# The first two x tiles of a fused attention and FFN kernel: transposed by DMA instead of on TensorE

## The chip, the cores and the metric

The kernel runs on one core of one Trainium2 chip. Its time is the device time of one execution in microseconds. Before the change three runs took 249.02, 248.76 and 249.07 us, a median of 249.02 us.

## The reference

The input `x` has 2048 rows of 1024 bf16 values. Two blocks work on it, and a gate per row mixes their results:

```
g   = sigmoid(sum(x * gate_w))                      # one number per row
qkv = x @ wqkv                                      # 1024 -> 3 * 1024, 32 heads of 32
pq, pk = phi(q), phi(k)                             # phi(t) = (t + 1 if t > 0 else exp(t)) + 1e-6
kv  = sum over rows of pk^T v, z = sum over rows of pk      # per head
a   = (pq @ kv / (pq . z + 1e-6)) @ wo              # linear attention
i   = argmax over rows of x @ w_r
b   = x, with sigmoid(x[i] @ w_r) * ((silu(x[i] @ w_gate) * (x[i] @ w_up)) @ w_down) added to row i
out = g * a + (1 - g) * b
```

So K and V are needed for all rows before any output can be made, and one single row goes through the FFN.

## The kernel before

The 2048 rows are 16 tiles of 128 (`NT`), the 1024 columns of `x` are 8 chunks of 128 (`KC`). TensorE contracts over the partitions, so every product with `wqkv` needs `x` transposed: `xT[p, c, s]` holds column `128 c + p` of row `s`. For K and V a 128x128 block of `xT` is the stationary operand and 512 (K) or about 350 (V) columns of the weights `wkv` stream past it. For Q it is the other way round.

The order of the stages:

1. Start-up: `wkv` comes in row by row of chunks. `load_k(c)` brings the K columns of chunk c, 256 KB each. The first two x tiles are worked on with the K rows as these arrive: `first_mm(t, c, c + 1)` makes the two 512-column matmuls (`first` in the profile) of tile t with K row c. The loop below `first_mm(0, 0, 1)` goes over c and alternates: row c for tile 0, then row c - 1 for tile 1.
2. `unit_V(t, 2)`: the last third of V, together with the two router columns (`w_r` and `gate_w`, put into `wkv` by way of the tile `wps`), for tiles 0 to 3 and then, after K of tile 2, for tiles 4 to 15.
3. From tile 4 on, a loop of K, the rest of V, and Q for later tiles; the sums over rows (`unit_KVACC`), the FFN of the one selected row, and at the end the output tiles.

Who brings x where it is needed: tiles 0 and 1 are loaded as they are by `load_x` (a plain DMA of 256 KB each, to `xnat`) and transposed on TensorE by `unit_T`. That makes eight 128x128 transposes per tile into two PSUM tiles (`pst`), and copies one of these to `xT` on VectorE (DVE) and one on ScalarE (ACT). Tiles 2 and 3 each come by one DMA that transposes on the way (`sp.dma_start_transpose`), tiles 4 to 15 by three such DMAs of four tiles each.

What sets the order: the kernel is written with a tile framework that puts in the semaphores. `in_order` (lines 78 to 90) wraps the calls of an engine, so that instructions keep the order of the program on TensorE, DVE, ACT and SP. The wrapper is why most lines of the profile read L83, and tiles are told apart by their names. All large loads are issued by SP in this order: x tile 0, x tile 1, K rows 0 to 7, the last third of V for all chunks in one DMA (640 KB, behind `v_cut`), the transposing DMAs of tiles 2, 3, 4-7, 8-11 and 12-15, the rest of V in two DMAs, and the Q weights. From K row 4 on, an issue also waits until an earlier DMA has landed, since their landing semaphores are used in turn: K row 7 and the V third wait for the load that SP issued eight DMAs earlier. ACT issues two small loads of 2 KB for the router columns at the start.

While TensorE waits for data it runs dummy matmuls on a constant (`warm`, tile `warm_ps`): six of 512 columns at the start (`N_WARM`), two of 128 behind `wps`, four of 128 behind the second `unit_T`. Their result is not used. The start-up on TensorE is written out like this:

```
unit_T(0)
wps = ...                       # router columns: transpose, copy into wkv
warm(2, 128)
unit_T(1)
warm(4, 128)
first_mm(0, 0, 1)
for c in range(1, KC):
    first_mm(0, c, c + 1)
    if c < KC - 1:
        first_mm(1, c - 1, c)
```

Of the kernel before, what the change touches and what calls it, by code (L numbers as in the profile page):

```python
# [13 lines left out]
BF = mybir.dt.bfloat16  # L14
# [8 lines left out]
P = 128  # L23
S = 2048
D = 1024
F = 3584
NT = S // P
KC = D // P
NG = D // P
EPS = 1e-6  # L30
LN1EPS = math.log1p(EPS)
N_WARM = 6
Q_PER_T = {4: 2, 5: 1, 6: 1, 7: 2, 8: 2, 9: 1, 10: 2, 11: 1, 12: 1, 13: 1, 14: 1, 15: 1}
VH = (11, 11, 10)
REDUCE_AFTER = {(6, 3): 0, (9, 4): 1}
# [10 lines left out]
def kernel(  # L46
# [14 lines left out]
    x2d = A_x.rearrange("b s d -> (b s) d")  # L61
    out2d = out.rearrange("b s d -> (b s) d")
    wqkv_v = A_wqkv.rearrange("(c p) n -> p c n", p=P)
    x_v = x2d.rearrange("(t p) d -> p t d", p=P)
# [13 lines left out]
    def in_order(engine, names, own=(False,)):  # L78
        last = [None]

        def wrap(fn):
            def call(*a, **k):
                inst = fn(*a, **k)  # L83
                if last[0] is not None and (strict[0] or own[0]):
                    tc.add_manual_dep(inst.ins, last[0].ins.name, NOSYNC, reason="program order on this engine")
                last[0] = inst
                return inst

            return call

        return SimpleNamespace(**{n: wrap(getattr(engine, n)) for n in names})

    pe = in_order(nc.tensor, ["matmul", "transpose"])
    dve = in_order(nc.vector, ["memset", "tensor_copy", "tensor_scalar", "tensor_scalar_add", "tensor_tensor", "scalar_tensor_tensor",
                               "reciprocal", "max", "max_index", "tensor_reduce", "stream_shuffle"], strict_dve)
    sp = in_order(nc.sync, ["dma_start", "dma_start_transpose"])
    act = in_order(nc.scalar, ["activation", "copy"])
# [11 lines left out]
    xT = pa.tile([P, KC, S], BF)  # L109
# [6 lines left out]
    ps_t = ps_t_cm.__enter__()  # L116
# [5 lines left out]
    xin_cm = tc.tile_pool(name="xin", bufs=2)  # L122
    xin = xin_cm.__enter__()
    wrg_rows = xin.tile([16, P], BF, name="wrg_rows", bufs=1)
    xnat = {}

    def load_x(t0, n):
        xt4 = xin.tile([P, n, D], BF, name=f"xnat{t0}", bufs=1)
        sp.dma_start(out=xt4[:, 0:n, :], in_=x_v[:, t0 : t0 + n, :])
        for i in range(n):  # L130
            xnat[t0 + i] = xt4[:, i, :]

    def load_k(c):
        sp.dma_start(out=wkv[:, c, 0:D], in_=wqkv_v[:, c, D : 2 * D])

    load_x(0, 1)
    load_x(1, 1)
    for c in range(KC):
        load_k(c)
    v_cut = D + 32 * (VH[0] + VH[1])  # L140
    sp.dma_start(out=wkv[:, :, v_cut : 2 * D], in_=wqkv_v[:, :, D + v_cut : 3 * D])
# [9 lines left out]
    ident = const.tile([P, P], BF)  # L151
# [34 lines left out]
    def phi_exp(ps):  # L186
        u = tmp.tile([P, 512], F32, tag="phi_u")
        act.activation(u[:], ps, ACTF.Relu, scale=-1.0, bias=LN1EPS)
        e = tmp.tile([P, 512], F32, tag="phi_e")
        act.activation(e[:], u[:], ACTF.Exp, scale=-1.0, bias=LN1EPS)  # L190
        return e

    def phi_dve(ps, e0, out_ap):
        dve.scalar_tensor_tensor(out_ap, ps, EPS, e0[:], op0=ALU.max, op1=ALU.add)

    def phi_evac(ps, out_ap):
        phi_dve(ps, phi_exp(ps), out_ap)

    def unit_T(t):
        for h, eng in enumerate((dve.tensor_copy, act.copy)):  # L200
            pst = ps_t.tile([P, 512], BF, tag="t")
            for c in range(4):
                pe.transpose(pst[:, c * P : (c + 1) * P], xnat[t][:, (4 * h + c) * P : (4 * h + c + 1) * P], ident[:])
            eng(xT[:, 4 * h : 4 * h + 4, t * P : (t + 1) * P], pst[:].rearrange("p (c s) -> p c s", c=4))

    pk_t = {}
    vt_t = {}
# [1 line left out]
    def kv_open(t):  # L209
        if t not in pk_t:  # L210
            pk_t[t] = kvp.tile([P, D], BF, tag="pk", name=f"pk{t}")
            vt_t[t] = kvp.tile([P, VH[0] + VH[1], 33], BF, tag="vt", name=f"vt{t}")
            nc.gpsimd.memset(vt_t[t][:, :, 32:33], 1.0)  # L213

    def kv_mm(ps, t, nb, c0, c1):
        for c in range(c0, c1):
            pe.matmul(ps[:], lhsT=xT[:, c, t * P : (t + 1) * P], rhs=wkv[:, c, 512 * nb : 512 * nb + 512],
                             start=(c == 0), stop=(c == KC - 1))
# [43 lines left out]
    def warm(n, w=512):  # L262
        for _ in range(n):
            pe.matmul(warm_ps[:, 0:w], lhsT=warm_w, rhs=warm_x[:, 0:w], start=True, stop=True)

    warm(N_WARM)
    kv_open(0)
# [3 lines left out]
    def first_mm(t, c0, c1):  # L271
        for c in range(c0, c1):
            for nb in range(2):
                kv_mm(first[t][nb], t, nb, c, c + 1)

    unit_T(0)
    wps = ps_t.tile([P, 16], BF, tag="t")
    pe.transpose(wps[:], wrg_rows[:], ident[0:16, 0:16])
    dve.tensor_copy(wkv[:, :, 2 * D : 2 * D + 2], wps[:].rearrange("p (w c) -> p c w", w=2))
    warm(2, 128)  # L280
    unit_T(1)
    warm(4, 128)
    first_mm(0, 0, 1)
    for c in range(1, KC):
        first_mm(0, c, c + 1)
        if c < KC - 1:
# [455 lines left out]
```

## Time and profile before

| | us |
|---|---|
| median of 3 runs | 249.02 |
| the profiled execution | 249.02 |
| its span, first to last instruction | 247.4 |
| TensorE busy (matmuls) | 241.0 (97%) |
| VectorE (DVE) busy | 172.7 (70%) |
| ScalarE (ACT) busy | 127.7 (52%) |
| GpSimd (POOL) busy | 52.7 (21%) |
| DMA moved | 47.78 MB, mean 193 GB/s |

The profile is one execution, recorded by the hardware. A line of instructions gives the line of the kernel, the engine, the operation, the tiles (out<-in), how many, and times. PE is TensorE's matmuls, PEld its weight loads, which run beside them. "SPq" is the queue of SP, which only issues DMAs; of a DMA the trace gives when it was issued, how long the issue held the queue, and how long after the issue it had landed. The chain is the work that ended last, followed back step by step to whatever released it. The packets of the core's 16 DMA engines are recorded one by one, so the rate in any stretch can be asked for. Matmuls overlap in the pipeline: a single one's duration (379 ns for 512 columns) is longer than the distance from one start to the next, and it is this distance, the pitch, that tells TensorE's pace.

### The profile page before, as it was taken

What the parts mean: (1) busy time and instruction counts of PE and PEld (TensorE: products, weight loads), DVE (VectorE), ACT (ScalarE), POOL (GpSimd) and SP (SyncE); (2) the same over time, 40 slices, a digit from 0 to 9 for tenths busy, and PEclk for the clock granted to TensorE, in tenths of its full rate; (3) what the DMA queues carried; (4) which work ended last, traced back from release to release, by engine and by line L of the source; (5) the groups of instructions that cost most, each with busy time, mean ns of one, the idle gap of its engine ahead of it and who ended that gap; (6) DMA issues with size and microseconds to landing.
All of it is one profiled execution on the core that took longest, in us unless ns stands there. A gap on an engine that the chain in (4) does not pass through costs nothing.

```text
span 247.4 us, 4873 instructions
## 1 busy us (share of the span) xinstructions
PE 241.0 (97%) x1901; PEld 124.3 (50%) x1926; DVE 172.7 (70%) x264; ACT 127.7 (52%) x215; POOL 52.7 (21%) x100
## 2 busy tenths in 40 slices
PE   8999999999999999999999999999999999999994
PEld 4466756654554554554554555544443444444442
DVE  1053124379985979845989999996789999954342
ACT  3095344455566466545555555668887633333300
POOL 6000000400000100000013300101666689950000
PEclk9999999999999999999999999999999999999999
DMA  6999994499969993599659891000003654565122
GB/s 212 339 243 200 273 396 127 106 337 335 269 193 300 342 290 79 153 326 391 205 164 455 286 243 48 3 4 21 0 3 127 200 184 149 152 190 168 47 83 86
DMA packets 46311, 47.78 MB, mean 193 GB/s; under 512 B 16776, under 2 KB 35472, under 8 KB 46224
## 3 DMA queue, kind: packets, MB, share of 16 engines
q1 hardware_dynamic: 45648, 46.28, 61.0%
q0 software_dynamic: 608, 1.19, 1.8%
q8 instruction: 15, 0.25, 0.4%
q14 instruction: 8, 0.07, 0.1%
q10 hardware_dynamic: 32, 0.00, 0.0%
HBM read 39.33 MB, written 8.39 MB: 193 GB/s over the span
## 4 chain that ended last, share of the span: by engine, by line
PE 97%; issue 1%; DVE 0%; DVEq 0%
PE ps L83 88%; PE first L83 3%; PE kvacc L83 2%; PE warm_ps L83 1%; PE red L83 1%; PE pst L83 1%; PE dps L83 1%; PE pm L83 1%; DVE ot L83 0%; PE yps L83 0%; DVEq L737 0%; PE pt L83 0%; PE hps L83 0%; PE rps L83 0%; PE wps L83 0%
## 5 line engine op out<-in xcount | busy, mean ns | idle before, releaser
L83 PE MATMUL ps<-wkv,xT 128*128 128x352 bf16 (+2 forms) x600 | 106.1, 334 | 0.4
L83 PEld LDWEIGHTS <-xT 128*128 128x128 bf16 x640 | 62.3, 98 | 49.3 <-issue 0.5
L83 ACT ACTIVATE u<-ps 128x512 f32<-128x512 f32 x60 | 35.9, 598 | 46.4 <-PE ps L83 46.2
L83 PE MATMUL ps<-xT,wq 128*128 128x512 bf16 x246 | 57.6, 379 | 0.7 <-issue 0.3
L83 PE MATMUL ps<-m_sb,pq_all 128*128 128x512 bf16 (+2 forms) x258 | 55.1, 372 | 0.4 <-issue 0.2
L83 ACT ACTIVATE e<-u 128x512 f32<-128x512 f32 x64 | 40.3, 630 | 2.1
L83 PEld LDWEIGHTS <-pq_all 128*128 128x128 bf16 x264 | 25.4, 98 | 30.2 <-issue 0.7
L640 POOL TENSOR_TENSOR pq_all<-pq_all,rb 128x512 bf16<-128x512 bf16 x32 | 36.5, 1170 | 12.1 <-DVE rb L83 11.7
L83 PEld LDWEIGHTS <-wq 128*128 128x128 bf16 x256 | 24.4, 98 | 28.4 <-issue 1.4
L83 DVE SCALAR_TENSOR_TENSOR gacc<-wt,hcol,gacc 128x1024 f32<-128x1024 bf16 x27 | 34.5, 1279 | 0.4
L83 DVE SCALAR_TENSOR_TENSOR ot<-ps,gate,xg 128x512 bf16<-128x512 f32 (+2 forms) x33 | 24.0, 738 | 14.3 <-PE ps L83 14.2
L83 DVE SCALAR_TENSOR_TENSOR gacc<-wt,xs_f,gacc 128x2048 f32<-128x2048 bf16 x14 | 32.8, 2345 | 0.2
L83 ACT ACTIVATE xg<-xt,omg 128x1024 f32<-128x1024 bf16 x16 | 18.1, 1146 | 26.8 <-DVE ot L83 25.9
L83 DVE SCALAR_TENSOR_TENSOR pq_all<-ps,e 128x512 bf16<-128x512 f32 x32 | 21.9, 686 | 11.3 <-ACT e L83 11.3
L83 DVE SCALAR_TENSOR_TENSOR pk<-ps,e 128x512 bf16<-128x512 f32 x28 | 19.0, 686 | 11.8 <-ACT e L83 11.8
L83 DVE STREAM_SHUFFLE rb<-rdp 128x512 f32<-128x512 f32 x32 | 22.8, 752 | 0.0
L83 ACT CAST vt<-ps 128x352 bf16<-128x352 f32 x32 | 14.4, 454 | 11.4 <-PE ps L83 11.1
L213 POOL MEMSET vt<- 128x22 bf16 x16 | 3.8, 440 | 75.7 <-PE kvacc L83 75.3
L83 ACT CAST vc<-ps 128x320 bf16<-128x320 f32 x16 | 6.5, 429 | 7.3 <-PE ps L83 7.3
L83 DVE COPY rg<-ps 128x2 f32<-128x2 f32 x16 | 2.5, 159 | 10.2 <-ACT vc L83 10.1
L355 POOL DMA_DIRECT2D xs<-in_A_x_dram x1 | 0.7, 711 | 39.5 <-DVE sig L83 39.5
L83 DVE SCALAR_TENSOR_TENSOR pk<-first,e 128x512 bf16<-128x512 f32 x4 | 2.8, 692 | 9.0 <-ACT e L83 9.0
(100 smaller groups left out, 96.1 us busy)
## 6 DMA issues: line engine op xcount, KB each, us to landing
wt<-in_B_w_down_dram SPq DMA_DIRECT2D x14, 512.0 KB, 4.6
wt<-in_B_w_gate_dram SPq DMA_DIRECT2D x8, 512.0 KB, 7.6
wt<-in_B_w_up_dram SPq DMA_DIRECT2D x8, 512.0 KB, 7.4
xt<-xp SPq DMA_DIRECT2D x16, 256.0 KB, 2.7
out_dram<-ot SPq DMA_DIRECT2D x15, 256.0 KB, 2.0
wt<-in_B_w_gate_dram SPq DMA_DIRECT2D x8, 384.0 KB, 8.0
wt<-in_B_w_up_dram SPq DMA_DIRECT2D x8, 384.0 KB, 6.9
wkv<-in_A_wqkv_dram SPq DMA_DIRECT2D x8, 256.0 KB, 4.6
```

The lines of the kernel that those rows point to most:

```text
L83: inst = fn(*a, **k)
L213: nc.gpsimd.memset(vt_t[t][:, :, 32:33], 1.0)
L355: nc.gpsimd.dma_start(out=xs8[:], in_=x2d[bass.ds(idx_val, 1), :].rearrange("o (c p) -> (o c) p", p=P))
L640: nc.gpsimd.tensor_tensor(sl, sl, rb[:], op=ALU.mult)
```

## The change

The first two x tiles also come by transposing DMAs (`load_xt`), straight into `xT`; `load_x`, `xnat` and `unit_T` are gone. SP's order becomes: x tile 0, K row 0, x tile 1, K rows 1 to 7, and then as before. On TensorE the 16 transposes and the four dummies behind them are gone, `N_WARM` is 8 instead of 6, and the two matmuls of K row 0 with tile 0 stand ahead of the `wps` transpose and its two small dummies. The copies from PSUM to `xT` on DVE and ACT are gone as well.

```diff
-N_WARM = 6
+N_WARM = 8
...
-    def load_x(t0, n):
-        xt4 = xin.tile([P, n, D], BF, name=f"xnat{t0}", bufs=1)
-        sp.dma_start(out=xt4[:, 0:n, :], in_=x_v[:, t0 : t0 + n, :])
-        for i in range(n):
-            xnat[t0 + i] = xt4[:, i, :]
...
-    load_x(0, 1)
-    load_x(1, 1)
-    for c in range(KC):
+    def load_xt(t):
+        sp.dma_start_transpose(out=xT[:, :, t * P : (t + 1) * P], in_=x2d[t * P : (t + 1) * P, :])
+
+    load_xt(0)
+    load_k(0)
+    load_xt(1)
+    for c in range(1, KC):
         load_k(c)
...
-    def unit_T(t):
-        for h, eng in enumerate((dve.tensor_copy, act.copy)):
-            pst = ps_t.tile([P, 512], BF, tag="t")
-            for c in range(4):
-                pe.transpose(pst[:, c * P : (c + 1) * P], xnat[t][:, (4 * h + c) * P : (4 * h + c + 1) * P], ident[:])
-            eng(xT[:, 4 * h : 4 * h + 4, t * P : (t + 1) * P], pst[:].rearrange("p (c s) -> p c s", c=4))
...
-    unit_T(0)
+    first_mm(0, 0, 1)
     wps = ps_t.tile([P, 16], BF, tag="t")
     pe.transpose(wps[:], wrg_rows[:], ident[0:16, 0:16])
     dve.tensor_copy(wkv[:, :, 2 * D : 2 * D + 2], wps[:].rearrange("p (w c) -> p c w", w=2))
     warm(2, 128)
-    unit_T(1)
-    warm(4, 128)
-    first_mm(0, 0, 1)
     for c in range(1, KC):
         first_mm(0, c, c + 1)
         if c < KC - 1:
```

More of the change, by code (lines that the diff above doesn't have):

```diff
@@ L124 @@
     wrg_rows = xin.tile([16, P], BF, name="wrg_rows", bufs=1)
-    xnat = {}
-    def load_x(t0, n):
-        xt4 = xin.tile([P, n, D], BF, name=f"xnat{t0}", bufs=1)
-        sp.dma_start(out=xt4[:, 0:n, :], in_=x_v[:, t0 : t0 + n, :])
-        for i in range(n):
-            xnat[t0 + i] = xt4[:, i, :]
     def load_k(c):
         sp.dma_start(out=wkv[:, c, 0:D], in_=wqkv_v[:, c, D : 2 * D])
-    load_x(0, 1)
-    load_x(1, 1)
-    for c in range(KC):
+    def load_xt(t):
[4 more added lines that the diff above has]
+    for c in range(1, KC):
         load_k(c)
```

## The prediction

> **What bounds the kernel now.** First the page: busy times and the chain that ended last.
>
> ```profile
> PE 241.0 (97%) x1901; PEld 124.3 (50%) x1926; DVE 172.7 (70%) x264; ACT 127.7 (52%) x215; POOL 52.7 (21%) x100
> ...
> PE 97%; issue 1%; DVE 0%; DVEq 0%
> ```
>
> TensorE is busy for 241.0 of 247.4 us and is 97% of the chain. Its matmul stream has no holes to speak of, so the end can move only by TensorE's start-up, by a new hole, or by its pace. All edits lie in the start-up, so the chain in order of time comes next (start, length, what):
>
> ```profile
> 0.98 0.04 issue
> 1.02 2.72 PE warm_ps L83 x6
> 3.74 1.01 PE pst L83 x8
> 4.75 0.12 PE wps L83
> 4.88 0.33 PE warm_ps L83 x2
> 5.20 0.85 PE pst L83 x8
> 6.06 0.43 PE warm_ps L83 x4
> 6.48 4.37 PE first L83 x20
> ```
>
> Two things are to be seen. Up to 6.48 us TensorE does only dummies and transposes: filler until the first K rows have landed. And its pace changes there: a 512-column dummy takes 2.72/6 = 0.45 us, a 512-column `first` matmul 4.37/20 = 0.218; a 128-column dummy 0.43/4 = 0.107, about half the 0.218 instead of a quarter. The array thus runs at half rate until about 6.5 us, after some 5.4 us of unbroken work, and at full rate from then on. (The clock column of the page shows full speed there too; the pitch is the better witness.)
>
> The stretches for the `first` matmuls alone (length, busy time, count):
>
> ```profile
> 6.28:6.80 0.52, 0.52 (x2) 0.00 (x0) 0.00 (x0) 1.00 1.18 323
> 6.80:13.28 6.48, 6.43 (x30) 0.00 (x0) 0.60 (x1) 1.00 1.10 322
> ```
>
> K row 0 takes two matmuls, to 6.80; from row 1 on, 30 matmuls run back to back at 6.48/30 = 0.216 us, and after 13.28 the V matmuls follow without a hole. When row 1 may start therefore sets the end of the kernel. The DMA issues tell when it may (issue to landing in us, one issue per line; issue times from the timeline: x tile 0 at 0.98, x tile 1 at 1.45, K row 0 at 1.91, K row 1 at 2.40, the last third of V at 5.76):
>
> ```profile
> xnat<-in_A_x_dram SPq DMA_DIRECT2D x1, 256.0 KB, 2.7
> ...
> xnat<-in_A_x_dram SPq DMA_DIRECT2D x1, 256.0 KB, 2.9
> ...
> wkv<-in_A_wqkv_dram SPq DMA_DIRECT2D x1, 256.0 KB, 3.8
> ...
> wkv<-in_A_wqkv_dram SPq DMA_DIRECT2D x1, 256.0 KB, 4.3
> ...
> wkv<-in_A_wqkv_dram SPq DMA_DIRECT2D x1, 640.0 KB, 7.1
> ```
>
> So x0 lands at 3.7, x1 at 4.35, K row 0 at 5.7, K row 1 at 6.7, 0.1 us before TensorE takes it at 6.80, and the V third at 12.9, 0.4 us before 13.28. The start-up is bound by one stream of bytes, x0, x1, K0, K1, and the transposes are hidden in its wait.
>
> **The change, part by part.** *Removed from TensorE:* 16 transposes (1.01 + 0.85 us of chain), four 128-column dummies (0.43). *Added:* two 512-column dummies. All of it is at half rate and before row 1. The eight dummies end at 1.02 + 8 x 0.43 = 4.5 us. *Row 0* moves ahead of the small `wps` transpose and needs only x0 and K0, no more x1. All this is worth nothing while K row 1 is the last to come: the 30 matmuls behind it take 6.48 us in either kernel. The most that row 0's own two matmuls can give is the 0.1 us between the landing at 6.7 and 6.80. The four copies out of PSUM (two on DVE, two on ACT) were on nobody's path: zero; their cover is the idle 7.6 us of DVE and 5.7 us of ACT before their first K work.
>
> *The x tiles by DMA transpose.* K1 now comes behind x0 (transposed), K0, x1 (transposed). It is the same 1 MB, so what counts is how fast it flows. The rows of the same trace where transposes flow, begin and end (windows 2 to 6, 12.25 to 12.75, 26.5 to 27.5, 27.6 to 28.8 and 29 to 32 us):
>
> ```profile
> DMA packets 698, 1.25 MB, mean 312 GB/s; under 512 B 91, under 2 KB 91, under 8 KB 698
> ...
> DMA packets 192, 0.05 MB, mean 98 GB/s; under 512 B 192, under 2 KB 192, under 8 KB 192
> ...
> DMA packets 1134, 0.29 MB, mean 290 GB/s; under 512 B 1134, under 2 KB 1134, under 8 KB 1134
> ...
> DMA packets 188, 0.13 MB, mean 108 GB/s; under 512 B 110, under 2 KB 188, under 8 KB 188
> ...
> DMA packets 824, 1.14 MB, mean 379 GB/s; under 512 B 16, under 2 KB 824, under 8 KB 824
> ```
>
> (a) Transposes in full flow move 290 GB/s in 256-byte packets: 0.90 us for a tile of 0.262 MB. Plain loads made 312 in this same start-up (0.84 us) and 379 at their best (0.69). Two tiles: +0.13 to +0.43 us; I take 0.2, nearer to the start-up's own row.
> (b) Going from plain loads to transposes, the stream fell to 98 GB/s for 0.5 us: 0.33 us lost against 290. After the change this happens once, K0 to x1: 0 to 0.33, I take 0.1, because there it fell into a full queue.
> (c) Going from transposes back to plain loads it fell to 108 GB/s for 1.2 us: 0.13 MB where 379 GB/s takes 0.34 us, 0.86 us lost. This happens twice ahead of K1 (x0 to K0, x1 to K1): 0 to 1.7 us. That row stands behind 3 MB of transposes and mine behind a quarter of one each, so I take half, 0.4 each, 0.8.
> (d) SP's issue. A plain issue takes 0.45 us. The two 128-row transposes took 4.05 and 1.76 us, behind a full queue. With an empty queue one costs between a plain 0.43 and 1.76. At 1.76, K1 is issued at 0.98 + 2 x 1.76 + 0.45 + three steps of 0.05 = 5.1 instead of 2.40, and with the shortest delay shown for 256 KB (2.7) lands at 7.8. This runs beside (a) to (c) and is not added: it only sets a floor of 7.8 at its upper end.
>
> Sum: 0.2 + 0.1 + 0.8 = 1.1, K1 lands at 7.8 instead of 6.7; less the 0.1 us of slack, row 1 starts 1.0 us late. Bounds: +0.1 - 0.1 = 0.0 at the low end, 0.43 + 0.33 + 1.72 - 0.1 = +2.4 at the high end.
>
> The Trainium skill speaks against the change: "VectorE: DVE Perf Modes", The three transpose paths, gives 1309 ns for one 128x128 block by DMA and 390 ns on TensorE, and its rules send a transpose whose result may go to PSUM to TensorE. A tile is eight blocks; one after the other that would be an estimated 10.5 us each, and K1 some 19 us late. This trace moves a tile in 0.90 us once transposes flow, so I don't expect that figure to hold here.
>
> *Queued behind.* On SP stand K2 to K7, the V third, then the transposes of the other x tiles; the later issues wait for landings of the earlier ones (K7's for K0, the third of V for x1). All were issued 4 to 7 us before they landed, so 1 us more of issue is covered. Their landings shift with the stream by about 1.1, their deadlines on TensorE by 1.0: the third of V keeps 0.3 of its 0.4 us, the transpose of x tiles 4 to 7 (issued 12.64, 7.8 to landing, 20.4, needed at 21.10) about 0.6. Zero, but thin. K rows land every 0.7 us and are used up every 4 x 0.216 = 0.86, so rows 2 to 7 do not bind.
>
> *The clock.* Before, TensorE worked without a pause from 1.02 until the pitch doubled near 6.5. After, it pauses from 4.5 until K0 is there (about 5.3: without x1 ahead, with (a) and (c) once), works for about 1.3 us and waits again until 7.8. If the pauses do not put the doubling off, this costs nothing, since row 1 starts later than 6.5: taken as 0. If the unbroken work has to begin anew at 7.8, full rate comes 5.4 us later and half of that is lost: +2.7 us. This is the upper bound.
>
> The Trainium skill, "TensorE: Matmul & The Clock Gate", Part 1, has the gate open after about 3.4 us of sustained work in a free-running window; eight dummies of 0.43 us just fill one. By that rule the clock may come as early as 4.5 us or as late as a further window of 3.4 us, an estimated loss of up to 1.7. The row, 5.4 us from first work to full pitch, fits a window that began at 3.0.
>
> **Total.** The profiled run took 249.02 us, the median of the three runs as well, with a span of 247.4 (1.6 lie around it). 249.02 + 1.0 = 250.0.
>
> **Rivals.**
> 1. *Clock late.* The pauses cost a further window of half rate: 1.0 plus 1.4 to 2.7, about 251.4 to 252.7. For it: nothing shows the clock rising over a pause. Against it: two thirds of the time to 6.5 stays busy.
> 2. *The issue binds, not the stream.* SP needs 1.76 us per transpose, (b) and (c) are small, and K1 lands at 7.8 by its issue alone: 250.0 again, but with idle DMA engines at 3 to 5 us. For it: the shortest transpose issue on record. Against: that one stood behind a full queue.
> 3. *Hidden anyway.* From an empty queue the transposes flow at once, nothing is lost at the turns, K1 lands at 6.8: 249.0 to 249.4.
> 4. *Faster.* K1 lands earlier than now. Before, the first microsecond of the stream ran at 260 GB/s, and K1's landing came a microsecond after its bytes' turn at the mean rate, which tells of engines out of step. If transposes keep them in step, K1 could land at 6.1 and row 1 start 0.6 us early: 248.4. It decides if K1 lands before 6.3. Against: the same bytes in smaller packets.
>
> **How the numbers follow.** Mine 0.36, the clock 0.26, issue 0.13, hidden 0.18, faster 0.07. About 0.5 us (0.2%) is what a measurement of this kernel tells from no change. Slower by more: 0.30 of mine (it reaches below 249.5 at its low bounds), all of the clock, 0.12 of issue, 0.05 of hidden, 0.73; within: 0.20; faster: 0.07. The range reaches from hidden (249.0) to most of the clock case (252.4). Without the clock case and the two that gain or hide it would be 249.3 to 251.4.
>
> **What would show it.** Right: no `pst` on TensorE, two holes in it before row 1 (near 4.5 to 5.3 and 6.3 to 7.8), K1 landing at 7.4 to 8.2, then a pitch of 0.216 and the V matmuls from about 14.3 without a hole. A pitch of 0.43 after row 1 shows rival 1; SP issues of 1.5 us or more and idle DMA engines rival 2; K1 at 6.8 rival 3. Wrong above all would be a first transpose with a set-up cost of its own, which no row here shows, or a hole at the third of V or at x tiles 4 to 7.

## The result, and the profile after

The changed kernel is slower: 255.08 us, the median of four runs (254.47 to 255.52), against 248.98 us (248.76 to 249.07). The ratio is 1.0245, with a 95% interval of 1.0219 to 1.0271, or +6.1 us. The prediction was 250.0 with a range up to 252.4: right in direction, far too small. The profiled execution took 255.52 us; its span is 254.0 where it was 247.4, so 6.6 us have to be found.

The page of the changed kernel, busy time of TensorE and the engines' shares of the chain:

```profile
PE 242.5 (95%) x1884; PEld 123.1 (48%) x1908; DVE 171.9 (68%) x262; ACT 126.6 (50%) x213; POOL 52.6 (21%) x100
...
PE 94%; DMA 2%; SPq 1%; issue 1%; DVE 0%; DVEq 0%
```

TensorE has 17 fewer recorded matmuls and is busy for 1.5 us more. The chain now has 2% of DMA and 1% of SP's queue in it, which were not there. Both point at the start-up, so the chain of the changed kernel in order of time (start, length, what):

```profile
0.98 1.36 SPq L83
2.35 0.06 issue
2.41 0.56 SPq L83
2.97 0.05 issue
3.02 1.24 SPq L83
4.26 0.04 issue
4.31 5.22 DMA wkv<-in_A_wqkv_dram
9.53 0.04 issue
9.57 9.23 PE first L83 x30
18.80 4.59 PE ps L83 x33
```

TensorE no longer starts this chain. SP does: 1.36 us to issue the transpose of x tile 0, 0.56 for K row 0, 1.24 for the transpose of x tile 1, so that K row 1 is issued at 4.31 instead of 2.40. It lands at 9.53 instead of 6.7. Then the 30 `first` matmuls behind it, as the stretches of the changed kernel for these alone show (length, busy time and count on TensorE, DVE and ACT, the clock, DMA share, GB/s):

```profile
9.57:14.86 5.29, 5.29 (x13) 0.00 (x0) 0.00 (x0) 0.50 1.21 307
14.86:18.64 3.78, 3.78 (x18) 0.00 (x0) 0.60 (x1) 1.00 1.05 235
```

They take 9.07 us instead of 6.48: up to 14.86 one starts every 0.42 us, from there every 0.22 (the one on the border is counted in both stretches). V starts at 18.64 instead of 13.28. One more piece lies far from the change. TensorE's timeline of the changed kernel (start, length, what, the idle time before in brackets):

```profile
90.36 0.39 PE L83 MATMUL ps<-xT,wq 128*128 128x512 bf16 x1
91.86 1.47 PE L83 MATMUL ps<-xT,wq 128*128 128x512 bf16 x6 [1.12 <-issue]
```

The same seven matmuls in the timeline of the kernel before stand in one piece:

```profile
84.89 1.90 PE L83 MATMUL ps<-xT,wq 128*128 128x512 bf16 x7
```

In the middle of a group of eight accumulating matmuls for Q, right behind the 128 short matmuls of `unit_KVACC` for tiles 4 to 7, TensorE stands still for 1.12 us (one of the eight has no record in either profile). The releaser is given as issue: it waits for no semaphore.

The account is then, measured as the shift of the same instructions against the kernel before:

| piece | us |
|---|---|
| row 1 starts at 9.57 instead of 6.80 | +2.77 |
| half clock in the `first` matmuls, 9.07 instead of 6.48 | +2.59 |
| hole at 90.75 (the shift goes from 5.36 to 6.53 across it) | +1.17 |
| sum, of 6.6 in the span | +6.53 |

### The profile page after: what moved, and what is told of

Same layout as the page of the kernel before. It is cut to its first block, busy times and chain, and to the rows that moved or that the text cites. A ratio compares the mean times of both kernels' runs of the same rounds, so it can differ in the third digit from the quotient of the medians.

```text
span 254.0 us, 4831 instructions
## 1 busy us (share of the span) xinstructions
PE 242.5 (95%) x1884; PEld 123.1 (48%) x1908; DVE 171.9 (68%) x262; ACT 126.6 (50%) x213; POOL 52.6 (21%) x100
## 4 chain that ended last, share of the span: by engine, by line
PE 94%; DMA 2%; SPq 1%; issue 1%; DVE 0%; DVEq 0%
PE ps L83 85%; PE first L83 4%; DMA wkv<-in_A_wqkv_dram 2%; PE kvacc L83 2%; SPq L83 1%; PE red L83 1%; PE dps L83 1%; PE pm L83 1%; DVE ot L83 0%; PE yps L83 0%; DVEq L723 0%; PE pt L83 0%; PE hps L83 0%; PE rps L83 0%; PE xs_ps L83 0%
## 5 line engine op out<-in xcount | busy, mean ns | idle before, releaser
L83 DVE SCALAR_TENSOR_TENSOR ot<-ps,gate,xg 128x512 bf16<-128x512 f32 (+2 forms) x33 | 23.9, 735 | 14.3 <-PE ps L83 14.2
L83 PE MATMUL first<-wkv,xT 128*128 128x512 bf16 x32 | 9.8, 475 | 4.1 <-DMA wkv<-in_A_wqkv_dram 4.1
```

## The experiments

Three questions follow: why K row 1 lands so late, what costs the clock, and where the hole comes from. The edits are against the changed kernel or the one before, as said. Each ratio is against runs of the kernel before on the same chip; its medians there were 249.13 (runs e1 to e4), 249.12 (e5 to e8) and 249.43 (e9 to e12). What the profiles show, in us:

| kernel | K1 issued | K1 landed | row 1 starts | half rate until | V starts | hole | span |
|---|---|---|---|---|---|---|---|
| before | 2.40 | 6.7 | 6.80 | 6.5 | 13.28 | none | 247.4 |
| after | 4.31 | 9.53 | 9.57 | 4.6, and 8.03 to 14.86 | 18.64 | 1.12 | 254.0 |
| e1 after again | 4.31 | 8.18 | 8.22 | 3.9, and 7.32 to 14.14 | 17.60 | 1.30 | 253.1 |
| e2 bridge | 4.31 | 8.96 | 9.65 | 6.7 | 16.13 | none | 250.3 |
| e3 plain x | 2.40 | 7.03 | 7.07 | 5.3 | 13.54 | 1.27 | 248.8 |
| e4 late K1 | 2.87 | 11.01 | 11.06 | 6.2, and 9.64 to 16.46 | 20.18 | none | 253.9 |
| e5 longer list | 4.31 | 8.89 | 8.94 | 14.05 | 17.92 | none | 252.1 |
| e6 both x first | 4.37 | 8.32 | 10.54 | 5.5 | 17.01 | none | 251.2 |
| e7 small packets | 3.04 | 7.46 | 7.51 | 5.6 | 13.98 | 1.23 | 249.4 |
| e8 rows first | 2.4 | 7.00 | 7.19 (row 0 at 6.33) | 5.4 | 13.23 | none | 247.2 |
| e9 K by ACT | 1.4 | 4.99 | 6.56 | 5.2 | 13.88 | 1.37 | 249.0 |
| e10 list of before shifted | 2.40 | 7.23 | 7.27 | 6.5 | 13.74 | 1.44 | 249.2 |
| e11 mended | 4.37 | 8.30 | 8.46 | 3.8 | 14.96 | none | 249.1 |
| e12 before again | 2.39 | 7.01 | 7.07 | 7.0 | 13.76 | none | 247.8 |

### e1: the changed kernel again

No edit.

> The changed kernel once more, for a second profile. In its first profile K row 1 landed at 9.53 us (one DMA engine held a single 2 KB packet for 2.0 us; the other 15 engines were done by 8.1), the clock was full from 4.62 to 8.03, half until 14.86. Theory (late K row 1, and a clock lost in the pause): K row 1 lands between 8.0 and 9.6 again, and the pitch of the matmuls behind it is 0.43 us for some us, with the moment of the change elsewhere, as the clock's windows need not begin at the same place; 254.4 to 255.5 us. Rival (the one held packet is the cause): without it K row 1 lands at 8.1 and the time is about 253.5.

Measured: 254.23 us (253.17 to 254.79), ratio 1.0188 [1.0155, 1.0221]. The median is 5.1 us above that of the kernel before, a microsecond less than in the first four runs. K row 1 was again issued at 4.31 but landed at 8.18, 1.35 us earlier than in the first profile, where one DMA engine held a single 2 KB packet for 2.03 us while the other fifteen were done by 8.11. V gained only 1.04 us of this, for the clock came back at nearly the same time (14.14 against 14.86). The account closes as before: 1.42 for row 1, 9.38 - 6.48 = 2.90 for the clock, 1.30 for the hole, 5.62 in sum of 5.7.

### e2: dummies until K row 1 is there

```diff
-N_WARM = 8
+N_WARM = 14
...
-    warm(2, 128)
+    warm(10)
```

> The changed kernel with its pauses filled: 14 dummies of 512 columns at the start instead of 8, and 10 of 512 columns instead of 2 of 128 behind row 0 (0.216 us each at full clock). Theory (the pause loses the clock): the clock stays full from its first rise on, the 30 matmuls of rows 1 to 7 run at 0.216 us, and 2.6 us come back: 252.4, still 3 above before because K row 1 is late. Rival (the clock does not depend on the pauses, or the half pitch is the data's): no change, 255. If K row 1 should land at 8.1, the ten dummies end later (about 8.7) and cost 0.6 of it.

Measured: 251.56 us (251.13 to 251.86), 1.0087 [1.0068, 1.0105]. The stretch of the `first` matmuls from row 1 on in e2:

```profile
9.65:16.13 6.48, 6.42 (x29) 0.00 (x0) 0.60 (x1) 1.00 1.11 301
```

With no pause the clock is not lost, and the 30 matmuls take 6.48 us, exactly as before the change. The whole 2.6 to 2.9 us of the second item is thus the clock's answer to TensorE's pauses. Row 1 waits here for dummies that overran the landing by 0.7 us. The hole is gone too, which no theory on the start-up explains; it led to e5.

### e3: the same order of loads, x tiles plain

The first two tiles stay untransposed here; POOL copies them to `xT` for later use.

```diff
     def load_xt(t):
-        sp.dma_start_transpose(out=xT[:, :, t * P : (t + 1) * P], in_=x2d[t * P : (t + 1) * P, :])
+        xnat[t] = xin.tile([P, KC, P], BF, name=f"xnat{t}", bufs=1)
+        sp.dma_start(out=xnat[t][:], in_=x_v[:, t, :].rearrange("p (c s) -> p c s", c=KC))
...
-            pe.matmul(ps[:], lhsT=xT[:, c, t * P : (t + 1) * P], rhs=wkv[:, c, 512 * nb : 512 * nb + 512],
+            pe.matmul(ps[:], lhsT=xnat[t][:, c, :] if t < 2 else xT[:, c, t * P : (t + 1) * P], rhs=wkv[:, c, 512 * nb : 512 * nb + 512],
...
+    for t in range(2):
+        nc.gpsimd.tensor_copy(xT[:, :, t * P : (t + 1) * P], xnat[t][:])
```

> The changed kernel with both x tiles loaded as plain 2 KB rows in the same places of the queue, and used untransposed by the first matmuls (GpSimd copies them to xT for later; the result is not the reference's, since tiles 0 and 1 are not transposed). Same order, same dummies, same matmuls, only the DMA transposition is gone. Theory (the transposing DMAs delay the stream): K row 1 lands at 6.7 to 7.0 instead of 9.5, the pauses shrink to about 0.5 us each, and the time falls to 249 to 250. Rival (order, removed filler or the SP queue cost the time): 252 or more.

Measured: 251.43 us (250.38 to 253.0), 1.0108 [1.0062, 1.0155]; the profiled run is the 250.38. The chain of e3:

```profile
2.40 4.63 DMA wkv<-in_A_wqkv_dram
7.03 0.04 issue
7.07 6.63 PE first L83 x30
```

With plain loads K row 1 is issued at 2.40 again and lands at 7.03. So it is the transposing DMAs that make it late, neither the order x0, K0, x1, K1 nor the missing work on TensorE. Two pauses of TensorE are there as well, but row 1 comes early enough to end them, and the clock stays. Of the 1.4 us that the span has over 247.4, V's shift is 0.26; the rest is the hole, which is here without any transpose of these two tiles by DMA.

### e4: K row 1 late without any transposing DMA

Against the kernel before:

```diff
-    for c in range(KC):
+    load_k(0)
+    scratch = xin.tile([P, 4, D], BF, name="scratch", bufs=1)
+    sp.dma_start(out=scratch[:], in_=x_v[:, 8:12, :])
+    for c in range(1, KC):
         load_k(c)
```

> The kernel before, with TensorE's transposes and all dummies, and an additional plain load of 1 MB into a tile that nothing reads, put between K row 0 and K row 1. K row 1 lands some 2.8 us later with no DMA transpose near it. Theory: TensorE pauses from 6.8 to about 9.5; the shift is 2.8 if the clock survives the pause and up to 5.5 if it is lost, 252 to 254.5; the pitch behind K row 1 tells which. If DMA transposes cost something beyond the late landing, this kernel stays clearly below the changed one's 255.1 at the same landing time.

Measured: 255.46 us (255.12 to 255.96), 1.0250 [1.0228, 1.0272]. The megabyte in front cost 4.3 us, not 2.8: K row 1 landed at 11.01. The windows of e4 between the moments at which the clock may move (length, then busy time and count on PE, PEld, DVE, ACT, POOL, the clock, DMA share, GB/s):

```profile
6.22:9.64 3.42, 0.64 (x5) 0.24 (x4) 0.00 (x0) 0.48 (x1) 0.00 (x0) 1.00 0.98 370
9.64:13.05 3.41, 1.99 (x5) 0.69 (x5) 0.00 (x0) 0.00 (x0) 0.00 (x0) 0.50 1.06 398
13.05:16.46 3.41, 3.41 (x9) 1.18 (x8) 0.00 (x0) 0.00 (x0) 0.00 (x0) 0.50 1.24 244
```

The clock goes to half and stays there for two windows, as in the changed kernel, with every transpose of tiles 0 and 1 still on TensorE. A late K row 1 is enough to lose it.

### e5: 36 more entries in TensorE's list

The changed kernel has 18 matmuls fewer than the kernel before, each with its weight load, so TensorE's instruction list is 36 entries shorter. In e2, which has 14 dummies more than the changed kernel, it is only 8 shorter. Eighteen dummies of 16 columns, each a weight load and a matmul, bring the changed kernel back to the length of before:

```diff
+    warm(18, 16)
     warm(N_WARM)
```

> The changed kernel with 18 dummies of 16 columns put ahead of the eight, so that TensorE's instruction list has the length of the kernel before again (36 entries more). The changed kernel (both profiles) and the plain-x kernel have a hole of 1.1 to 1.3 us in TensorE in the middle of an accumulation group, 8 instructions behind the 128 small kvacc matmuls of tiles 4 to 7 (at 87 to 92 us), which no semaphore explains; before, the bridged and the late-K kernel, whose lists are longer, have none. Theory (instructions arrive late there, and the place depends on how many came before): the hole is gone, 1.2 us come back, about 253.2 (K row 1 at 8.2 to 9.5 and the clock as in the changed kernel). Rival (the hole belongs to the shifted schedule of DVE and the weight stream): it stays, 254.3.

Measured: 253.74 us (253.61 to 253.88), 1.0182 [1.0166, 1.0197]. TensorE's timeline of e5 at the place of the hole:

```profile
89.34 0.26 PE L83 MATMUL kvacc<-vc,pk 128*32 128x33 bf16 x10
89.54 1.90 PE L83 MATMUL ps<-xT,wq 128*128 128x512 bf16 x7
```

The hole is gone; the late K row 1 and the clock are not. Here the clock did not rise at all before 14.05, V starts at 17.92, between the 17.60 and 18.64 of the two profiles of the changed kernel, and its shift of 4.64 is all of the 4.7 that the span has over 247.4.

### e6: both x tiles ahead of the K rows, with the bridge

The edit of e2, and:

```diff
     load_xt(0)
-    load_k(0)
     load_xt(1)
+    load_k(0)
```

> The bridged kernel with both x tiles transposed ahead of K row 0 (x0, x1, K0, K1 in the queue), so that the stream turns from transposes to plain rows once ahead of K row 1, not twice, and from plain to transposes not at all. In the bridged kernel K row 1 landed at 8.96. Theory (the turns cost): one turn and one alignment of the DMA engines less, K row 1 at 7.9 to 8.2 and K row 0 at 7.2 to 7.5. If the dummies end in time the total falls by the same 0.8 to 1.0, otherwise it stays at 251.5, as they end near 9.6 when the clock rises late. Rival (only the issue time or the small packets cost): K row 1 lands at 8.9 as before.

Measured: 252.73 us (252.41 to 253.16), 1.0142 [1.0123, 1.0160]. K row 1 landed at 8.32, a little later than the theory's 7.9 to 8.2, and 3.95 us after its issue. Row 0 came later with it, the ten dummies behind row 0 ran to 10.54, and the kernel lost there more than it gained. As a test of the time it says little; its landing is used below.

### e7: the small packets alone

Pieces of 256 bytes, but issued as a plain DMA, so that the two tiles stay untransposed:

```diff
-        sp.dma_start_transpose(out=xT[:, :, t * P : (t + 1) * P], in_=x2d[t * P : (t + 1) * P, :])
+        sp.dma_start(out=xT[:, :, t * P : (t + 1) * P], in_=x_v[:, t, :].rearrange("p (c s) -> p c s", c=KC))
```

> The changed kernel with the x tiles loaded by plain DMAs straight into xT, a row as eight pieces of 256 bytes: the same order, the same packet size and the same 1024 packets per tile as a transposing DMA, but no transposition (the result is not the reference's, since tiles 0 and 1 stand untransposed). Theory (it is the transposing that costs: the engines wait for each other at its start, and plain rows are slow behind it): K row 1 lands near the 7.0 of the plain kernel, 7.0 to 7.5. Rival (the small packets cost): 8.2 or more. The instruction list is the changed kernel's, so the hole near 87 us should be there: 250.5 to 251.5 if the clock survives the pauses, up to 2.7 more if not.

Measured: 251.65 us (250.88 to 254.09), 1.0129 [1.0080, 1.0178]. The chain of e7, from a run of 250.91 us:

```profile
3.04 4.43 DMA wkv<-in_A_wqkv_dram
7.46 0.04 issue
7.51 6.63 PE first L83 x30
```

K row 1 is 0.43 us later than in e3, with its issue 0.64 later; counted from its issue it took less, 4.43 against 4.63. Packets of 256 bytes thus explain at most 0.43 of the 1.15 to 2.5 us between e3 and the changed kernel, and K row 1 scatters by as much with plain loads alone (6.7 to 7.23 in the profiles of before, e8, e10 and e12). The rest belongs to the transposing form of the DMA.

### e8: row by row in the kernel before

If K row 1 binds, both tiles' matmuls of row 0 could fill the time ahead of it:

```diff
-    warm(4, 128)
+    warm(4, 16)
     first_mm(0, 0, 1)
+    first_mm(1, 0, 1)
     for c in range(1, KC):
         first_mm(0, c, c + 1)
         if c < KC - 1:
-            first_mm(1, c - 1, c)
+            first_mm(1, c, c + 1)
     es = [phi_exp(first[0][nb][:]) for nb in range(2)]
-    first_mm(1, 6, 8)
+    first_mm(1, 7, 8)
```

> The kernel before with one idea of the study turned into a gain: both tiles take K row 0 before K row 1 (and then each row for both tiles), and the four 128-column dummies ahead of them shrink to 16 columns. 28 instead of 30 matmuls then stand behind K row 1. If K row 1 (6.7 us) is what binds, row 0 of both tiles ends at about 7.0 and the V matmuls start at 13.0 instead of 13.3: 248.8, a gain of 0.2 to 0.3 us, hardly more than can be measured. Rival: the third of V, which lands at 12.9, becomes the bound, or the clock rises later because there is less filler: 249.0 to 249.5.

Measured: 249.0 us (248.74 to 250.77, eleven runs) against 249.12 (fifteen runs): 0.9999 [0.9982, 1.0016], no difference. The gain of 0.2 to 0.3 us that was expected lies within this interval, so it is not ruled out. In the profile K row 0 landed at 6.29 instead of 5.74, and it, not K row 1, decided when V starts (13.23).

### e9: K rows 0 and 1 issued by ACT

Against the changed kernel, so that they do not stand behind SP's transposes:

```diff
-        sp.dma_start(out=wkv[:, c, 0:D], in_=wqkv_v[:, c, D : 2 * D])
+        (nc.scalar if c < 2 else sp).dma_start(out=wkv[:, c, 0:D], in_=wqkv_v[:, c, D : 2 * D])
```

> The changed kernel with K rows 0 and 1 issued by ACT, so that they do not wait behind SP's issues of the two transposes (1.36 and 1.24 us, which put K row 1's issue at 4.31 instead of 2.40). Theory (the issue on SP is the smaller part, what flows behind a transpose is the larger): K row 1, now issued at about 1.5 and mixed in among the transposes, lands at 6.5 to 7.5, but x tile 1 lands late instead, at 7.5 or more, and the matmuls of tile 1 wait for that: the first V matmul moves by less than 1 us against the changed kernel. Rival (the issue binds): both K row 1 and x tile 1 are in by 7.2, and the time falls to 251 with the hole near 87 us, or to 253 if the clock is lost in the pauses all the same.

Measured: 252.49 us (250.53 to 253.33), 1.0143 [1.0114, 1.0172]. The profile is of the fastest run, 250.53. All packets of 2 to 6.5 us in e9:

```profile
DMA packets 2527, 1.25 MB, mean 277 GB/s; under 512 B 2176, under 2 KB 2176, under 8 KB 2527
```

The same stretch of the changed kernel, with as many small packets:

```profile
DMA packets 2308, 0.85 MB, mean 190 GB/s; under 512 B 2149, under 2 KB 2149, under 8 KB 2308
```

And of the kernel before:

```profile
DMA packets 782, 1.40 MB, mean 312 GB/s; under 512 B 98, under 2 KB 98, under 8 KB 782
```

The DMA issues of e9, K row 1 (issued at 1.39) and x tile 1 (issued at 2.40):

```profile
wkv<-in_A_wqkv_dram ACTq DMA_DIRECT2D x1, 256.0 KB, 3.6
...
xT<-in_A_x_dram SPq DMA_TRANSPOSE x1, 4.1
```

In e9 K row 1 lands at 4.99 and x tile 1, the last of the same megabyte, at 6.47, as early as K row 1 does in the kernel before (6.7). The theory that the transposes slow the stream itself had x tile 1 at 7.5 or later, and fell. With the K rows beside them, two transposes came in as early as plain loads do. The edit does two things at once: K row 1 is issued 2.9 us earlier, and it no longer stands behind the transposes in the same queue. How the two share the gain is not separated by it. The kernel gains less than its early K row 1 promises: row 1 starts at 6.56, but the third of V, now later on SP, lands at 13.83 and V begins at 13.88, and the hole of 1.37 us is there. The other three runs, without a profile, took 1.6 to 2.8 us more than this one. Why stays open in the main, as it does for the spread of e3 and e7 (2.6 and 3.2 us). TensorE pauses in all three, so the clock is suspected. The slowest run of e3 (253.0) and one of e9 (252.81) had a mean granted clock of 0.993, which is what one stretch of 3.41 us at half clock takes from 251. The other slower ones had 0.997 to 0.999; that does not clear them, since the column does not see a late first rise (e5: 1.000, at half rate until 14.05).

### e10: the list of the kernel before shifted

Against the kernel before, 116 tiny dummies in place of six long ones: 220 entries more than before, and so 256 more than in the changed kernel.

```diff
-    warm(N_WARM)
+    warm(116, 16)
```

> The kernel before with its six dummies of 512 columns replaced by 116 of 16 columns, about the same time: no DMA is changed, and 220 entries more stand in TensorE's list, which is 36 fewer than one full piece of 256 entries of 64 bytes (16,384 bytes, the size of the packets on the instruction queue). Theory (the hole near 87 us comes from where the pieces of the instruction list end): the hole of 1.1 to 1.3 us appears here too, in the same place behind the kvacc matmuls, with plain x tiles and all. Rival (it needs the late weight stream of the changed kernel): no hole. The small dummies may also let the clock rise later, so the time itself is not the measure.

Measured: 250.89 us, one run. TensorE's timeline of e10:

```profile
85.37 0.39 PE L83 MATMUL ps<-xT,wq 128*128 128x512 bf16 x1
87.19 1.47 PE L83 MATMUL ps<-xT,wq 128*128 128x512 bf16 x6 [1.44 <-issue]
```

The hole appears at the same matmul in the kernel before. Against e12 on the same chip V starts at 13.74 instead of 13.76, and the span is 1.4 us longer: the hole is the whole of it. These are one profile each, but apart from the dummies the two kernels are the same: neither a transposing DMA nor a late K row is needed for the hole, only another length of TensorE's list.

### e11: the change, mended

Both x tiles first, TensorE kept busy with dummies that do not overrun, and a list as long as in e2:

```diff
-N_WARM = 8
+N_WARM = 18
...
     load_xt(0)
-    load_k(0)
     load_xt(1)
+    load_k(0)
...
-    warm(2, 128)
+    warm(6, 16)
```

> The changed kernel with what the study found mended: both x tiles transposed ahead of K row 0, 18 dummies of 512 columns at the start so that TensorE hardly pauses, six small ones behind row 0, and a list as long as the bridged kernel's. Theory: K row 1 at 8.3 as in the run with both first, the clock full from its first rise, no hole: 1.5 to 1.9 above before, 250.6 to 251.0. If the clock is lost again, 253.5. If it comes to 249.2, the delay of K row 1 is not what is left.

Measured: 250.72 us (250.52 to 250.88), 1.0061 [1.0040, 1.0082]. The stretch of the `first` matmuls in e11:

```profile
8.46:14.96 6.50, 6.45 (x29) 0.00 (x0) 0.60 (x1) 1.00 1.11 308
```

No hole, no lost clock, and still 1.3 to 1.5 us slower: row 1 starts at 8.46, 1.66 later than 6.80. What is left is the late K row 1: against e12 V starts 1.20 later, and the span is 1.3 longer.

### e12: the kernel before, beside e9 to e11

No edit; a profile from the same chip.

> The kernel before for a second profile, to see how much its own K row 1 varies: landed at 6.71 in the first. Expected 6.6 to 7.1, no pause of TensorE ahead of row 1 longer than 0.4 us, full clock between 5 and 8 us and never lost, 248.8 to 249.6. If K row 1 lands at 8 here too, the late landings of the changed kernel are not the transposes'.

Measured: 249.41 us, one run. V starts at 13.76 and there is no hole, 0.48 us later than in the first profile: two profiles of this one kernel differ by that much in the start-up. K row 1 landed at 7.01, and K row 2, at 8.11, held TensorE up for another 0.2 us.

## Why the prediction was right or wrong

**Right.** The direction, and its reason: K row 1 is the last to come and comes later. No `pst`, and two pauses before row 1 (1.39 us up to 5.99 and 2.67 up to 9.57). In the changed kernel no load made a hole at the V third or at tiles 4 to 7, but the zero for what stands behind on SP was luck at the V third: it landed at 15.48, later than the 14.3 at which the prediction had V start, and was covered only because V started at 18.64. For the copies on DVE and ACT nothing is left in the account. Rivals 3 and 4 are out: K row 1 at 8.2 to 9.5 is neither 6.8 nor under 6.3, and even e11, with everything else mended, is slower.

**Row 1's delay, 1.0 predicted: mis-sized, and put on the wrong terms.** It was 2.77 us in the first profile and 1.42 in e1; the stated upper bound was 2.4. Term (a), small packets, taken as 0.2, cost at most 0.43 (e7 against e3), no more than the scatter. Terms (b) and (c), 0.9 for the turns between transposes and plain loads, are not a fixed price of a turn, but the fall of (c) is there. The packets of the microsecond behind the last one of x1, in e1, e7 and e9:

```profile
DMA packets 48, 0.10 MB, mean 96 GB/s; under 512 B 1, under 2 KB 1, under 8 KB 48
...
DMA packets 209, 0.39 MB, mean 385 GB/s; under 512 B 21, under 2 KB 21, under 8 KB 209
...
DMA packets 163, 0.31 MB, mean 307 GB/s; under 512 B 13, under 2 KB 13, under 8 KB 163
```

In e1 K rows 1 to 3 had been issued by then, and still the stream fell to 96 GB/s; in the other five profiles with K row 1 behind x1's transpose on SP's queue it made 121 to 260. Against the 385 behind the plain pieces of e7 that loses 0.3 to 0.75 us, where (c) took 0.4 a turn. In e9, where K row 2 follows x1 on SP, it did not fall; why is open. The step that failed is (d), "runs beside (a) to (c) and is not added: it only sets a floor". The issue times were 1.36 and 1.24 us, well inside the bounds given, and K row 1 was issued 1.9 us late. But a floor with the shortest delay on record, 2.7, was wrong, because its own delay stayed at 3.9 to 5.2 us:

```profile
xT<-in_A_x_dram SPq DMA_TRANSPOSE x1, 3.5
...
xT<-in_A_x_dram SPq DMA_TRANSPOSE x1, 3.9
...
wkv<-in_A_wqkv_dram SPq DMA_DIRECT2D x1, 256.0 KB, 5.2
```

These are the DMA issues of the changed kernel, x0, x1 and K1, with the time from issue to landing. While SP was issuing, the stream had little to move (190 GB/s instead of 312 over 2 to 6.5 us), and when K row 1 was issued at last, x1's packets were still ahead of it. Late issue and queueing add up: the prediction's own line for K row 1, 4.3 us from issue to landing, gives 4.31 + 4.3 = 8.6, and the four profiles with that issue time have 8.18, 8.89, 8.96 and 9.53. The sentence "the same 1 MB, so what counts is how fast it flows" held only as long as the queue was full. Rival 2 named the issue as the limit, with idle DMA engines, and was nearest to the mechanism, but priced it with the same floor. Why the delay varies from 3.9 to 5.2 is open; in the longest case one packet of 2 KB was held for 2.03 us.

The Trainium skill, "VectorE: DVE Perf Modes", Rules for kernel authors, sends such transposes to TensorE, and the direction agrees, even for e11 at +0.6%. The 1309 ns for a 128x128 block by DMA, under The three transpose paths, do not: eight blocks in a row would be an estimated 10.5 us, and a whole tile had landed 3.5 and 3.9 us after its issue.

**The clock, taken as 0: measured 2.59.** This is rival 1, given a chance of 0.26 and a price of 1.4 to 2.7, so the size was about right (2.90 in e1) and the choice was wrong. The sentence that failed is "if the pauses do not put the doubling off, this costs nothing, since row 1 starts later than 6.5". The pauses did not put it off; the clock rose early, at 4.62, and fell back at 8.03. That a pause may take away a clock already granted was in no step. The windows of the changed kernel, by the same columns as for e4:

```profile
1.20:4.62 3.42, 3.39 (x8) 1.01 (x7) 0.00 (x0) 1.28 (x1) 3.04 (x34) 1.00 0.63 120
4.62:8.03 3.41, 0.92 (x5) 0.36 (x5) 0.17 (x1) 0.00 (x0) 0.49 (x5) 1.00 1.09 270
8.03:11.45 3.42, 1.88 (x5) 0.69 (x5) 0.00 (x0) 0.00 (x0) 0.00 (x0) 0.50 0.94 317
11.45:14.86 3.41, 3.41 (x9) 1.18 (x8) 0.00 (x0) 0.00 (x0) 0.00 (x0) 0.50 1.33 293
```

The first row's 1.00 in the clock column is again not to be trusted: its dummies have a pitch of 0.45. The stretches are all 3.41 us, and each one's busy time fits what the clock does at its end: after 3.39 it rises, after 0.92 it falls, after 1.88 it does not rise, after 3.41 it does. Row 1 at 9.57 falls into a stretch too empty to count, so a whole further one is needed. That is why e1, e5 and the first profile, with row 1 at 8.2, 8.9 and 9.6, all regain the clock at 14.0 to 14.9. The windows of e1 show it with other amounts:

```profile
3.90:7.32 3.42, 1.34 (x7) 0.45 (x6) 0.17 (x1) 0.00 (x0) 1.22 (x7) 1.00 0.96 211
7.32:10.73 3.41, 2.51 (x7) 0.86 (x6) 0.00 (x0) 0.00 (x0) 0.00 (x0) 0.50 1.05 350
10.73:14.14 3.41, 3.41 (x9) 1.22 (x8) 0.00 (x0) 0.00 (x0) 0.00 (x0) 0.50 1.25 344
```

The Trainium skill, "TensorE: Matmul & The Clock Gate", Part 1, gives the free-running window of 3413 ns, and the traces agree. It has the clock go back after at least one idle window; here it fell after windows that were 19 to 39% busy (0.64, 0.92 and 1.34 of 3.41 us), and the measurement decides.

**The hole, in no step: 1.17.** The prediction named a hole at a load. This one hangs on the length of TensorE's list, as e5 and e10 show from both sides. The 36 entries that the change takes away were counted as work removed, and not as a shift of all the entries behind them.

**The range.** The two upper bounds in the text, 2.4 and 2.7, make 5.1 together, 254.1; the range ended at 252.4, since the lost clock was put on top of the 1.0 of the sum (rival 1), not on top of a K row 1 at its upper bound. They are one mechanism: e4 shows the clock lost because row 1 is late. A cause and its consequence have to be added, at their upper ends too. The hole was in neither bound.

## What to carry to other kernels

A load that costs its queue two to three times as much to issue delays all that is behind it on that queue, and the transfer time then comes on top: count the issue of each DMA ahead of the one that binds, and put that one ahead of them or on another queue. In a start-up that ends in full-rate matmuls, a late load is also a pause, and a pause can cost the clock for up to two windows of 3.41 us, so price the two together. When a change alters the number of instructions on TensorE, look through the whole trace for a new hole with no semaphore before looking for its reason near the edit.

## What the runs showed of the hardware

- The clock moves only at steps of 3.41 us. Over the profiles here it rose after stretches with 2.75 us of TensorE work or more, with one exception of 2.79 (e5, filled in part with tiny dummies); it did not rise after 2.68 or less. Once up, it fell in the start-up after 1.34 or less and was kept after 2.11 (e6) or more; at the end of the kernel it was kept after 1.55 (e9, 244.14 to 247.55 us) and fell after 1.11 (e7, 244.51 to 247.92). So a pause costs by how it lies in the stretches, not by its length alone. The stretches nearest to the borders are those of e7 (rose, then kept), e5 (did not rise) and e6 (kept), with length, busy time and count of TensorE, the clock, DMA share and GB/s:

```profile
2.17:5.58 3.41, 2.75 (x7) 1.00 0.89 222
5.58:8.99 3.41, 2.22 (x12) 1.00 1.01 352
...
3.81:7.22 3.41, 2.68 (x8) 1.00 0.99 201
...
5.49:8.90 3.41, 2.11 (x10) 1.00 0.94 316
```

- A hole of 1.1 to 1.4 us stands behind the second of four blocks of 128 matmuls of 33 columns (tiles 4 to 7) in the six profiles whose list is 36 entries shorter or 220 longer than that of the kernel before, and in none of the eight where it is as long or 8 shorter. The trace has the instruction fetch as packets of 16,384 bytes, 15 of them for the 3827 recorded instructions of TensorE in the kernel before, so about one per 256. In the six profiles such a packet begins 0.3 to 0.5 us after the block does and ends 0.1 to 0.2 us before the hole: in the changed kernel it runs from 89.46 to 90.61 and the hole begins at 90.75; in e10 from 84.50 to 85.58, the hole at 85.76. In the eight the last packet ahead of the block was over at least 1.4 us before the block began (81.16 and 83.54 in the kernel before). That TensorE used up short instructions faster than the next piece came fits this, but the packet ends before the hole begins, and what TensorE waits for in it was not shown. The Trainium skill, "Runtime: NRT & Kernel Launch", Instruction fetch mechanics, calls the cost of crossing such a boundary mostly hidden; if the hole is that cost, it was not hidden here.
- At the start of the kernel, SP's issue of a transposing DMA of 128 rows took 1.24 to 1.37 us, that of a plain 256 KB load 0.40 to 0.58 (0.57 and 0.71 for an x tile in pieces of 256 bytes, e7).
